# Partial sums of the first half leave PSUM through the four buffers of the weights' ring

## The chip, the cores and the metric

The kernel runs on one core of a Trainium2 chip. The metric is the time of one execution on the device, in microseconds (us). Before the change it is 872.65 us, the median of three runs (870.32, 872.65 and 874.05).

A core has these engines: TensorE (PE in the rows; PEld is its weight load), VectorE (DVE), ScalarE (ACT), GpSimd (POOL), and SyncE (SP), whose queue issues all DMAs here. Each engine carries out its own instructions in order; an instruction that waits for a semaphore holds all that stand behind it on that engine.

## The reference, cut to what matters

Sparse attention feeds two MLPs, one after the other, on 2304 tokens of width 512 with a hidden width of 2048:

```
x = attention(q, k, v)                          # 4 batches, 8 heads, 576 tokens, head width 64
h = x @ moe_w_in;  r = max(h, 0)
x = (moe_s * (r * r) + moe_b) @ moe_w_out       # first MLP
h = x @ moe2_w_in
g = h if h >= 1, 0 if h <= -1, else (h + 1)**2 / 4
out = g @ moe2_w_out                            # second MLP
```

The weights arrive as 64-bit floats and are decoded on the chip. Each fp32 operand of a product is split in a high and a low part (hi, lo), and each product is three matmuls: hi by hi, lo by hi, hi by lo.

## The kernel before, in words

The tokens are cut in six units of 384 (u = 0 to 5). The first MLP goes over the hidden width in two halves (`hf`), each of eight blocks of 128 (`m`). For one half, one unit and one block, `hidden` makes 12 matmuls into a PSUM tile `h` and a chain on ACT and DVE (relu L553, square L557 or L559, scale and shift L564 or L566, high part `gh` by the copy helper L282, low part `gl` L570). `output` makes 12 matmuls from `gh` and `gl` into four PSUM accumulators, three for each accumulator, in the order c = 0, 1, 2, 3. `output` of block m is issued two blocks behind `hidden` (LAG = 2), so on PE a group of 12 for `h` and a group of 12 for `acc` take turns.

The four accumulators (tags acc0 to acc3, one buffer each) hold the sum of one unit over the eight blocks of a half. Behind the last block of a unit in the first half, each is copied to SBUF by ACT (L282) or DVE (L284) into a tile `po` (L607, L608) and stored in DRAM as `part` (L609). Only then can the first matmul of the next unit write that accumulator. In the second half the parts are loaded back into tiles `pi` (L594) and added to the second half's sum (L613).

Behind the end of the attention (the list `lasts`), `prepare` makes the weights of the second MLP, beside the matmuls of the first. It decodes two blocks of weights (load L296, ACT L300, DVE L302, L304, L306) into tiles of the rings `qv` or `sm`, forms sums and differences of quarters (L365), and in `parts`, four times in each prepare, splits them: `hi` by ACT into a tile `pt` (L282), `lo` by DVE or POOL (L350); both are stored in DRAM as `dw` (L353). The first EARLY = 6 of the 16 prepares follow directly behind the attention, the others come in the second half.

Three rings of SBUF buffers matter here. `po` has PO = 2 buffers, `pi` has KD = 4, `pt` has PT = 2. A buffer is free when what was stored out of it has landed. Before the change `po` holds the parts of the first half and the low parts of the ten late prepares; `pi` holds the low parts of the six early prepares, and in the second half the parts that come back.

The order on each engine comes from a planner (`Issue.order`): every operation has a cost in us, a due time worked back from what needs it, and a fixed random jitter; the planner takes what can start first, then what is due first. An operation whose ring has no free buffer is not taken. A list given as `line=` (here `pi_line`) makes each of its operations start no earlier than the one before it on the list, which keeps the buffers of a ring in order.

Of the kernel before, what the change touches and what calls it, by code (L numbers as in the profile page):

```python
# [9 lines left out]
F32 = mybir.dt.float32  # L10
BF16 = mybir.dt.bfloat16
F32R = mybir.dt.float32r
# [10 lines left out]
KD = DM // 128  # L23
UNITS = [384] * 6
UMAX = max(UNITS)
# [17 lines left out]
RAW, DT, KB, QV, SM, PT, PO, TB = 3, 2, 4, 3, 3, 2, 2, 3  # L43
# [14 lines left out]
EARLY = 6  # L58
# [30 lines left out]
class Issue:  # L89
# [8 lines left out]
    def op(self, fn, engs, reads=(), writes=(), part=(), after=(), allocs=(), line=None):  # L98
        o = Op()
        o.fn, o.engs, o.n, o.succ, o.due = fn, engs, len(self.ops), [], None  # L100
        deps = set(after)
        o.behind, o.sooner = None, 0.0
        if line is not None:
            if line:
                o.behind = line[-1]
                deps.add(o.behind)
            line.append(o)
        for b in reads:
            deps.update(b.writers)
        for b in writes:  # L110
            deps.update(b.writers)
            deps.update(b.readers)
        for b in part:
            deps.update(b.readers)
        for b in reads:
            b.readers.append(o)
        for b in writes:
            b.writers, b.readers = [o], []
        for b in part:
            if b.readers:  # L120
                b.writers, b.readers = [], []
            b.writers.append(o)
        for b in allocs:
            b.writers = [o]
        o.deps = deps
        for d in deps:
            d.succ.append(o)
        o.bufs = [b for b in dict.fromkeys((*reads, *writes, *part, *allocs)) if b.ring]
        o.allocs = []
        for b in o.bufs:  # L130
            if not b.users:
                o.allocs.append(b)
                b.ring.made.append(b)
            b.users.append(o)
        self.ops.append(o)
        return o
# [85 lines left out]
def sparse_attention_two_mlps(ctx: ExitStack, tc: tile.TileContext, loc, strd, w_ins, w_outs, fixed, out):  # L222
# [5 lines left out]
    sp = ctx.enter_context(tc.tile_pool(name="sp", bufs=2))  # L228
# [19 lines left out]
    op = plan.op  # L248
# [4 lines left out]
    def buf(pool, tag, shape, dtype=F32, bufs=1):  # L253
        ring = rings.setdefault((pool.name if hasattr(pool, "name") else id(pool), tag), Ring(bufs))
        ring.name = tag
        serial[0] += 1
        name = f"{tag}_{serial[0]}"
        return Buf(ring, lambda: pool.tile(shape, dtype, tag=tag, name=name, bufs=bufs))


    def act(n):
        return ("act", 0.17 + n * 0.00062, 0.1)

    def dve(n, rate=0.00104):
        return ("dve", 0.07 + n * rate, 0.1)

    def dve2(n, rate=0.00104):

        return ("dve", 0.07 + n * rate, 0.1, "port")

    def pool(n):
        return ("pool", 0.1 + n * 0.0022, 0.1, "port")

    def dma(n, count=1):
        return ("sp", max(n / DMA_RATE, DMA_ISSUE * count), DMA_LATENCY)
# [4 lines left out]
    def copy(e, out, in_):  # L280
        if e is nc.scalar:
            e.activation(out=out, in_=in_, func=AF.Copy)  # L282
        else:
            e.tensor_copy(out=out, in_=in_)  # L284
# [4 lines left out]
    decodes, prepared, pi_line, w_loads, w0_line, w1_line = [], [], [], [], [], []  # L289
# [40 lines left out]
    def prepare(o, i):  # L330

        begin = len(plan.ops)
        src = w_outs if o else w_ins
        at = o * KP + i
        tag = ("qv", "sm")[at % 2]
        d1, d2 = (buf(sp, tag, [128, DM], I32, BUFS[tag]) for _ in range(2))
        _, x1, _, load = decode(src[2 * MS + i], lasts if at < EARLY else [*lasts, chain[0]], [d1, d2], d1)
        _, x2, *_ = decode(src[2 * MS + KP + i], [load], (), d2)
        where = {"A11": (d1, x1, 0), "A22": (d2, x2, 1)}
        where.update({"A21": (d1, x1, 1), "A12": (d2, x2, 0)} if o else {"A12": (d1, x1, 1), "A21": (d2, x2, 0)})  # L340

        def parts(b, f, k, names):
            n, q = 256 * len(names), [WMAT[name] for name in names]
            qs = slice(q[0], q[-1] + 1, max(q[-1] - q[0], 1))
            hi = buf(sp, "pt", [128, 512], F32R, PT)
            lo = buf(sp, "pi", [128, 512], F32R, KD) if at < EARLY else buf(sp, "po", [128, 512], F32R, PO)
            x = lambda: f()[:, k * 256:k * 256 + n]
            op(lambda e: copy(e, hi.tile[:, 0:n], x()), [act(n)], [b], [hi], allocs=[lo],
               line=pi_line if at < EARLY else None)
            op(lambda e: e.tensor_tensor(out=lo.tile[:, 0:n], in0=x(), in1=hi.tile[:, 0:n].bitcast(F32), op=SUB),  # L350
               [pool(n), dve2(n)], [b, hi], [lo])
            for w, y in enumerate((hi, lo)):
                op(lambda e, y=y, w=w: e.dma_start(  # L353
                    out=dw[o][i][qs, :, w, :].rearrange("q p n -> p q n"),
                    in_=y.tile[:, 0:n].bitcast(F32).rearrange("p (q n) -> p q n", n=256)), [dma(n * 512)], [y],
                   part=[dw_buf[o][i][v] for v in q])

        for names in [("A11",), ("A12", "A22")] if o else [("A11", "A12"), ("A22",)]:
            parts(*where[names[0]], names)

        for name, l, r, how in (("A22", "A21", "A22", ADD), ("A21", "A11", "A21", SUB), ("A11", "A22", "A11", SUB),
                                ("A12", "A12", "A11", SUB)):
            (b, f, k), (bl, fl, kl), (br, fr, kr) = (where[v] for v in (name, l, r))
            h = lambda f, k: f()[:, k * 256:(k + 1) * 256]
            op(lambda e, f=f, k=k, fl=fl, kl=kl, fr=fr, kr=kr, how=how: e.tensor_tensor(  # L365
                out=h(f, k), in0=h(fl, kl), in1=h(fr, kr), op=how), [dve2(256), pool(256)],
               [v for v in dict.fromkeys((bl, br)) if v is not b], [b])
        for names in [("S2", "S3"), ("S4", "S1")] if o else [("S2", "S4"), ("S3", "S1")]:
            parts(*((d1, x1) if names[0] == "S2" else (d2, x2)), 0, names)
        prepared.extend(plan.ops[begin:])  # L370
# [158 lines left out]
    def mm3(e, acc, w, x, first, last):  # L529
        (wh, wl), (ah, al) = w, x  # L530
        e.matmul(out=acc, lhsT=wh, rhs=ah, start=first, stop=False)  # L531
        e.matmul(out=acc, lhsT=wh, rhs=al, start=False, stop=False)  # L532
        e.matmul(out=acc, lhsT=wl, rhs=ah, start=False, stop=last)  # L533
# [4 lines left out]
    def pe_op(fn, n, reads, writes, allocs=()):  # L538
        chain[0] = op(fn, [pe(3 * (n / 2400 + 0.015))], reads, writes, after=[chain[0]] if chain[0] else (), allocs=allocs)
# [46 lines left out]
    def output(hf, u, m, g, gt):  # L586
        n = UNITS[u]
        w = wt[g, 1]
        cg = lambda: tuple(b.tile[:, 0:n] for b in gt)
        if hf == HF - 1 and m == 0:  # L590
            for c in range(KD):
                pin[c] = buf(sp, "pi", [128, UMAX], F32, KD)
                y = pin[c]
                op(lambda e, y=y, c=c: e.dma_start(out=y.tile[:, 0:n], in_=part_d[u][c]), [dma(n * 512)],  # L594
                   [part_buf[u][c]], [y], line=pi_line)
        for c in range(KD):
            if m == 0:
                acc[c] = buf(ps, f"acc{c}", [128, UMAX], F32, 1)
            a = acc[c]
            pe_op(lambda e, a=a, c=c: mm3(e, a.tile[:, 0:n], cut(w, c), cg(), m == 0, m == MS - 1), n, [*w, *gt], [a])  # L600
        if m < MS - 1:
            return
        line = []
        for c in range(KD):
            a = acc[c]
            if hf < HF - 1:
                y = buf(sp, "po", [128, UMAX], F32, PO)  # L607
                op(lambda e, y=y, a=a: copy(e, y.tile[:, 0:n], a.tile[:, 0:n]), [act(n), dve(n)], [a], [y])  # L608
                op(lambda e, y=y, c=c: e.dma_start(out=part_d[u][c], in_=y.tile[:, 0:n]), [dma(n * 512)],  # L609
                   [y], [part_buf[u][c]])  # L610
                continue
            y = pin[c]
            op(lambda e, y=y, a=a, c=c: e.tensor_tensor(out=x2[u].tile[:, c, :], in0=a.tile[:, 0:n], in1=y.tile[:, 0:n],  # L613
                                                        op=ADD),
               [dve(n)], [a, y], part=touched(u, c), allocs=[x2[u]] if c == 0 else (), line=line)
# [118 lines left out]
    n = NP  # L734
# [108 lines left out]
    at = 0  # L843
# [35 lines left out]
    for p in range(PAIRS):  # L879
        a = len(plan.ops)  # L880
# [110 lines left out]
```

## Time and profile before

| | |
|---|---|
| Median of three runs | 872.65 us (870.32 to 874.05) |
| Profiled execution | 872.29 us, its span 870.4 us |
| PE busy | 848.7 us (98%) |
| DVE, ACT busy | 663.5 us (76%), 533.9 us (61%) |
| Mean granted clock of TensorE | 0.984 of full speed |

The span runs from the first to the last instruction; 1.89 us of the profiled execution lie outside it. The attention's last matmuls are at about 170 us, the first half of the first MLP ends at about 323 us, the first MLP at about 517 us, and the second MLP takes the rest.

### The profile page before, as it was taken

How to read it: one execution, taken by the hardware profiler on the slowest of the kernel's cores; microseconds unless marked ns; L12 is line 12 of the kernel's file. 1: busy time of each engine (PE TensorE's matmuls, PEld its weight loads, DVE VectorE, ACT ScalarE, POOL GpSimd, SP SyncE). 2: the span in 40 equal slices, each digit the busy share in tenths (PEclk: the TensorE clock that was granted, in tenths of full speed). 3: DMA queues.
4: the chain of work that ended last, by engine and by line, in shares of the span. 5: the costliest groups of instructions: out<-in, count | busy, mean ns of one | idle time of the engine just before them, and what ended most of it. 6: DMA issues, size and time to landing. Idle time of an engine off the chain costs nothing.

```text
span 870.4 us, 15472 instructions
## 1 busy us (share of the span) xinstructions
PE 848.7 (98%) x5150; PEld 823.4 (95%) x5150; DVE 663.5 (76%) x1622; ACT 533.9 (61%) x1218; POOL 29.8 (3%) x43
## 2 busy tenths in 40 slices
PE   7799999998999999999999999999999999999998
PEld 4688898997999999999999999999999999999998
DVE  5899877588752892587988738899758998497966
ACT  5788776676654773566666635565555755465553
POOL 1112001000000000000000100000000000000000
PEclk9699999999899999999999999999999999999999
DMA  9568464478770560476878538888987888988783
GB/s 327 166 210 251 137 210 138 130 238 287 240 250 1 185 202 1 134 253 221 275 262 265 175 113 251 256 251 248 303 277 252 254 253 271 302 253 253 252 263 113
DMA packets 112591, 189.83 MB, mean 218 GB/s; under 512 B 11136, under 2 KB 54144, under 8 KB 112512
## 3 DMA queue, kind: packets, MB, share of 16 engines
q1 hardware_dynamic: 112512, 188.85, 67.9%
q8 instruction: 41, 0.67, 0.3%
q14 instruction: 38, 0.31, 0.1%
HBM read 150.00 MB, written 38.80 MB: 217 GB/s over the span
## 4 chain that ended last, share of the span: by engine, by line
PE 82%; DMA 8%; DVE 6%; ACT 2%; issue 1%; SPq 1%; DVEq 0%; ACTq 0%
PE acc L531 6%; PE acc L778 6%; PE h L531 6%; PE acc L779 6%; PE acc L777 6%; PE h L532 6%; PE h L533 6%; PE acc L532 6%; PE acc L533 6%; PE side L778 4%; PE side L779 4%; PE side L777 4%; PE h L778 3%; PE h L777 3%; PE h L779 3%; DMA raw<-in_w_ins 2%
## 5 line engine op out<-in xcount | busy, mean ns | idle before, releaser
L531 PE MATMUL acc<-gh,w1h 128*128 128x384 f32 x360 | 124.5, 346 | 5.8 <-ACT po L282 3.5
L532 PE MATMUL acc<-gl,w1h 128*128 128x384 f32 x360 | 121.2, 337 | 0.0
L533 PE MATMUL acc<-gh,w1l 128*128 128x384 f32 x360 | 121.1, 336 | 0.0
L531 PE MATMUL h<-xh,w0h 128*128 128x384 f32 x336 | 116.6, 347 | 0.0
L532 PE MATMUL h<-xl,w0h 128*128 128x384 f32 x336 | 114.4, 341 | 0.0
L533 PE MATMUL h<-xh,w0l 128*128 128x384 f32 x336 | 114.1, 339 | 0.0
L553 ACT ACTIVATE t<-h 128x384 f32<-128x384 f32 x96 | 46.4, 483 | 68.8 <-PE h L533 68.7
L531 PEld LDWEIGHTS acc<-gh,w1h 128*128 128x128 f32 x360 | 67.9, 189 | 8.6 <-ACT po L282 4.7
L532 PEld LDWEIGHTS acc<-gl,w1h 128*128 128x128 f32 x360 | 67.9, 189 | 0.1
L533 PEld LDWEIGHTS acc<-gh,w1l 128*128 128x128 f32 x360 | 67.8, 188 | 0.0
L531 PEld LDWEIGHTS h<-xh,w0h 128*128 128x128 f32 x336 | 64.3, 192 | 0.9 <-issue 0.5
L570 DVE TENSOR_TENSOR gl<-t,gh 128x384 fp32r<-128x384 f32 x92 | 51.0, 554 | 18.0 <-ACT gh L282 17.7
L532 PEld LDWEIGHTS h<-xl,w0h 128*128 128x128 f32 x336 | 64.4, 192 | 0.0
L533 PEld LDWEIGHTS h<-xh,w0l 128*128 128x128 f32 x336 | 64.2, 191 | 0.0
L566 DVE TENSOR_SCALAR t<-t,fix_t 128x384 f32<-128x384 f32 x58 | 29.7, 513 | 43.9 <-ACT t L557 43.7
L282 ACT ACTIVATE gh<-t 128x384 fp32r<-128x384 f32 x96 | 50.0, 521 | 18.3 <-DVE t L566 17.4
L282 ACT ACTIVATE gh<-w1h 128x384 fp32r<-128x384 f32 x60 | 31.6, 527 | 30.1 <-PE side L779 11.5
L456 ACT ACTIVATE sm<-sm,mx 128x96 f32<-128x96 f32 (+2 forms) x104 | 38.4, 372 | 11.2 <-DVE mx L446 10.9
L557 ACT ACTIVATE t<-t 128x384 f32<-128x384 f32 x76 | 39.8, 524 | 2.1
L819 DVE TENSOR_TENSOR gl<-w1h,gh 128x384 fp32r<-128x384 f32 x60 | 33.0, 553 | 6.7 <-ACT gh L282 6.7
L564 ACT ACTIVATE t<-t,fix_t 128x384 f32<-128x384 f32 x38 | 26.9, 708 | 3.2 <-DVE t L559 2.1
L282 ACT ACTIVATE pt<-sm 128x512 fp32r<-128x512 f32 (+1 forms) x32 | 18.2, 572 | 13.8 <-DVE sm L306 7.3
(342 smaller groups left out, 2342.7 us busy)
## 6 DMA issues: line engine op xcount, KB each, us to landing
w0h<-dw SPq DMA_DIRECT2D x168, 256.0 KB, 3.1
w0l<-dw SPq DMA_DIRECT2D x168, 256.0 KB, 3.1
raw<-in_w_ins SPq DMA_DIRECT2D x32, 512.0 KB, 5.0
raw<-in_w_outs SPq DMA_DIRECT2D x32, 512.0 KB, 4.5
dw<-pt SPq DMA_DIRECT2D x48, 256.0 KB, 3.1
dw<-po SPq DMA_DIRECT2D x30, 256.0 KB, 3.0
part<-po SPq DMA_DIRECT2D x24, 192.0 KB, 2.8
dw<-pi SPq DMA_DIRECT2D x18, 256.0 KB, 3.6
```

Source lines behind the costliest of these rows:

```text
L282: e.activation(out=out, in_=in_, func=AF.Copy)
L456: e.activation(out=sm.tile[0:nq, a, 0:nk], in_=sm.tile[0:nq, a, 0:nk], func=AF.Exp, scale=-1.0, bias=mx.tile[0:nq, a:a + 1], accum_out=dn. ...
L531: e.matmul(out=acc, lhsT=wh, rhs=ah, start=first, stop=False)
L532: e.matmul(out=acc, lhsT=wh, rhs=al, start=False, stop=False)
L533: e.matmul(out=acc, lhsT=wl, rhs=ah, start=False, stop=last)
L553: op(lambda e: e.activation(out=c(t), in_=c(p), func=AF.Relu), [act(n)], [p], [t])
L557: e.activation(out=c(t), in_=c(t), func=AF.Square)
L570: op(lambda e: e.tensor_tensor(out=c(gl), in0=c(t), in1=c(gh).bitcast(F32), op=SUB), [pool(n)] + [dve2(n)], [t, gh], [gl])
L777: e.matmul(out=dst, lhsT=wh, rhs=ah, start=opens and first, stop=False, skip_group_check=not opens)
L778: e.matmul(out=dst, lhsT=wh, rhs=al, start=False, stop=False, skip_group_check=not opens)
L779: e.matmul(out=dst, lhsT=wl, rhs=ah, start=False, stop=last, skip_group_check=not opens)
L819: op(lambda e, g=g, hi=hi, lo=lo: e.tensor_tensor(out=lo.tile, in0=g.tile, in1=hi.tile.bitcast(F32), op=SUB), [pool(n), dve2(n)], [g, hi], ...
```

## The change

The parts of the first half go into tiles of the ring `pi` (four buffers) and are put on `pi_line`. The low parts of the early prepares go into tiles of the ring `po` (two buffers), as those of the late ones do already, and leave `pi_line`. What is computed, the number of instructions and the sizes of all tiles stay.

```diff
@@ parts, in prepare @@
             hi = buf(sp, "pt", [128, 512], F32R, PT)
-            lo = buf(sp, "pi", [128, 512], F32R, KD) if at < EARLY else buf(sp, "po", [128, 512], F32R, PO)
+            lo = buf(sp, "po", [128, 512], F32R, PO)
             x = lambda: f()[:, k * 256:k * 256 + n]
-            op(lambda e: copy(e, hi.tile[:, 0:n], x()), [act(n)], [b], [hi], allocs=[lo],
-               line=pi_line if at < EARLY else None)
+            op(lambda e: copy(e, hi.tile[:, 0:n], x()), [act(n)], [b], [hi], allocs=[lo])
@@ output @@
             if hf < HF - 1:
-                y = buf(sp, "po", [128, UMAX], F32, PO)
-                op(lambda e, y=y, a=a: copy(e, y.tile[:, 0:n], a.tile[:, 0:n]), [act(n), dve(n)], [a], [y])
+                y = buf(sp, "pi", [128, UMAX], F32, KD)
+                op(lambda e, y=y, a=a: copy(e, y.tile[:, 0:n], a.tile[:, 0:n]), [act(n), dve(n)], [a], [y], line=pi_line)
                 op(lambda e, y=y, c=c: e.dma_start(out=part_d[u][c], in_=y.tile[:, 0:n]), [dma(n * 512)],
                    [y], [part_buf[u][c]])
```

Since the planner sees other rings, the order moves between the attention's last tiles and the end of the first half; outside of it the engines' rows stay. All lines behind L349 move up by one.

The first place is ACT at the end of unit 2 in the first half, near 210 us. There `acc_337` to `acc_340` are the accumulators c = 0 to 3 of that unit, `t` and `gh` belong to the chain of the next unit's blocks, `pt`, `sm` and `qv` to the prepares. Before:

```order
L300 ACTIVATE sm_2767<-raw_2766 128x512
L553 ACTIVATE t_2793<-h_2792 128x384
L282 ACTIVATE po_2828<-acc_337_2440 128x384
L557 ACTIVATE t_2793<-t_2793 128x384
L282 ACTIVATE po_2836<-acc_338_2447 128x384
L282 ACTIVATE pt_2842<-qv_2629 128x512
L282 ACTIVATE gh_2794<-t_2793 128x384
L282 ACTIVATE pt_2860<-qv_2630 128x512
L300 ACTIVATE sm_2768<-raw_2816 128x512
L553 ACTIVATE t_2848<-h_2847 128x384
L282 ACTIVATE po_2889<-acc_339_2456 128x384
```

Now:

```order
L300 ACTIVATE sm_2751<-raw_2750 128x512
L282 ACTIVATE pt_2805<-qv_2673 128x256
L552 ACTIVATE t_2792<-h_2791 128x384
L282 ACTIVATE pi_2828<-acc_337_2446 128x384
L556 ACTIVATE t_2792<-t_2792 128x384
L282 ACTIVATE pt_2838<-sm_2751 128x512
L282 ACTIVATE pi_2845<-acc_339_2458 128x384
L282 ACTIVATE pi_2856<-acc_340_2468 128x384
L282 ACTIVATE gh_2793<-t_2792 128x384
```

The copy of c = 2 stood behind the next block's relu and now stands two rows behind the copy of c = 0 and the square between them, with one `pt` copy ahead of it. The copy of c = 3 came from DVE and c = 1 from ACT; now it is the other way round.

The second place is DVE in the same stretch. The rows `pi<-..,pt` (before) and `po<-..,pt` (now) are low parts, `gl` is what PE waits for. Before, ahead of the end of unit 2:

```order
L350 TENSOR_TENSOR pi_2727<-sm_2395,pt_2726 128x512
L302 TENSOR_SCALAR qv_2630<-qv_2630 128x512
L350 TENSOR_TENSOR pi_2737<-sm_2396,pt_2736 128x512
L570 TENSOR_TENSOR gl_2692<-t_2690,gh_2691 128x384
L304 SCALAR_TENSOR_TENSOR qv_2630<-raw_2686,qv_2630 128x512
L306 SCALAR_TENSOR_TENSOR qv_2630<-raw_2686,qv_2630 128x512
L350 TENSOR_TENSOR pi_2775<-qv_2629,pt_2774 128x512
L566 TENSOR_SCALAR t_2741<-t_2741,fix_t 128x384
L350 TENSOR_TENSOR pi_2787<-qv_2630,pt_2786 128x256
```

Now, the closest run of low parts, ahead of the end of unit 3 (`acc_453` is its c = 1):

```order
L569 TENSOR_TENSOR gl_3098<-t_3096,gh_3097 128x384
L349 TENSOR_TENSOR po_3146<-qv_2968,pt_3145 128x512
L349 TENSOR_TENSOR po_3174<-qv_2967,pt_3173 128x512
L565 TENSOR_SCALAR t_3149<-t_3149,fix_t 128x384
L569 TENSOR_TENSOR gl_3151<-t_3149,gh_3150 128x384
L349 TENSOR_TENSOR po_3208<-sm_3038,pt_3207 128x256
L364 TENSOR_TENSOR sm_3038<-sm_3038 128x256
L364 TENSOR_TENSOR sm_3038<-sm_3037,sm_3038 128x256
L284 COPY pi_3231<-acc_453_2886 128x384
L364 TENSOR_TENSOR sm_3037<-sm_3038,sm_3037 128x256
L565 TENSOR_SCALAR t_3193<-t_3193,fix_t 128x384
L349 TENSOR_TENSOR po_3235<-sm_3038,pt_3234 128x512
```

A low part shares its buffer with the fourth one ahead of it before, and with the second one ahead of it now: `po_3208` with `po_3146`.

The third place is the SP queue at the end of the first half, where the last unit's parts are stored and the first parts are loaded back. Before:

```order
L609 DMA part_89<-po_3946 128x384
L699 DMA w0l_3973<-dw_1_91 128x512
L699 DMA w0h_3983<-dw_0_90 128x512
L609 DMA part_89<-po_3985 128x384
L699 DMA w0l_4003<-dw_1_91 128x512
L609 DMA part_89<-po_4005 128x384
L594 DMA pi_4245<-part_85 128x384
```

Now:

```order
L608 DMA part_89<-pi_3938 128x384
L608 DMA part_89<-pi_3945 128x384
L608 DMA part_89<-pi_3960 128x384
L593 DMA pi_3982<-part_84 128x384
L698 DMA w0l_3990<-dw_1_91 128x512
L593 DMA pi_3999<-part_84 128x384
L593 DMA pi_4006<-part_84 128x384
L593 DMA pi_4017<-part_84 128x384
L698 DMA w0h_4023<-dw_0_90 128x512
```

The four loads of unit 0's parts (`part_84`) stood among the early prepares, at about 247 to 252 us; they now follow the last stores, whose buffers they take.

## Rows read from the trace of the kernel before

**Rows 1.** The page, part 1: busy time, share of the span, instructions.

```profile
PE 848.7 (98%) x5150; PEld 823.4 (95%) x5150; DVE 663.5 (76%) x1622; ACT 533.9 (61%) x1218; POOL 29.8 (3%) x43
```

**Rows 2.** Waits of PE from 150 us: us in total, times, longest.

```profile
PE acc L531 <- ACT po L282: 3.5, 2, 3.3
PE acc L531 <- DVE po L284: 2.3, 2, 1.2
```

**Rows 3.** PE timeline: start, us, line, operation, out<-in, shape [idle before <- releaser].

```profile
196.47 0.34 PE L531 MATMUL h<-xh,w0h 128*128 128x384 f32 x1
...
200.63 0.34 PE L531 MATMUL h<-xh,w0h 128*128 128x384 f32 x1
...
207.06 0.34 PE L532 MATMUL acc<-gl,w1h 128*128 128x384 f32 x1
...
211.55 0.34 PE L533 MATMUL acc<-gh,w1l 128*128 128x384 f32 x1
...
215.97 0.44 PE L531 MATMUL acc<-gh,w1h 128*128 128x384 f32 x1 [3.28 <-ACT po L282]
...
217.82 0.69 PE L531 MATMUL acc<-gh,w1h 128*128 128x384 f32 x1 [1.07 <-DVE po L284]
...
223.68 0.34 PE L531 MATMUL acc<-gh,w1h 128*128 128x384 f32 x1
```

**Rows 4.** ACT and DVE timeline at the end of unit 2.

```profile
210.56 0.48 ACT L282 ACTIVATE po<-acc 128x384 f32<-128x384 f32 x1
210.93 0.53 ACT L557 ACTIVATE t<-t 128x384 f32<-128x384 f32 x1
211.34 0.49 ACT L282 ACTIVATE po<-acc 128x384 f32<-128x384 f32 x1
211.71 0.64 ACT L282 ACTIVATE pt<-qv 128x512 fp32r<-128x512 f32 x1
...
215.42 0.49 ACT L282 ACTIVATE po<-acc 128x384 f32<-128x384 f32 x1 [0.34 <-DMA part<-po]
...
217.21 0.56 DVE L284 COPY po<-acc 128x384 f32<-128x384 f32 x1 [1.32 <-DMA part<-po]
```

**Rows 5.** The chain that ended last, around 212 us: start, us, what.

```profile
211.86 5.25 DMA part<-po
```

**Rows 6.** Windows: us; PE, PEld, DVE, ACT, POOL busy; clock; DMA share; GB/s.

```profile
212.00:214.00 2.00, 0.68 (x3) 0.36 (x3) 2.00 (x5) 1.29 (x3) 0.00 (x0) 1.00 0.96 347
...
216.00:218.00 2.00, 0.93 (x4) 0.61 (x5) 0.79 (x2) 1.19 (x3) 0.00 (x0) 0.68 0.91 352
218.00:222.00 4.00, 4.00 (x13) 4.00 (x14) 3.79 (x9) 1.88 (x4) 0.00 (x0) 0.50 0.96 281
...
174.00:230.00 56.00, 51.64 (x279) 50.50 (x278) 46.89 (x94) 39.08 (x78) 0.00 (x0) 0.94 0.78 248
250.00:300.00 50.00, 48.52 (x278) 47.88 (x277) 23.43 (x44) 25.04 (x47) 0.00 (x0) 1.00 0.38 129
```

**Rows 7.** PE timeline at the ends of units 3 and 4.

```profile
253.76 0.44 PE L531 MATMUL acc<-gh,w1h 128*128 128x384 f32 x1 [0.24 <-ACT po L282]
...
288.61 0.44 PE L531 MATMUL acc<-gh,w1h 128*128 128x384 f32 x1 [1.24 <-DVE po L284]
```

**Rows 8.** DVE timeline: two low parts, two places apart, and a gl.

```profile
203.20 0.68 DVE L350 TENSOR_TENSOR pi<-sm,pt 128x512 fp32r<-128x512 f32 x1
...
204.85 0.55 DVE L570 TENSOR_TENSOR gl<-t,gh 128x384 fp32r<-128x384 f32 x1
...
206.65 0.68 DVE L350 TENSOR_TENSOR pi<-qv,pt 128x512 fp32r<-128x512 f32 x1
```

**Rows 9.** The tile pi from 174 to 232 us: issue to landing.

```profile
DMA to landing us min/median/max: 2.2/4.4/5.8
```

**Rows 10.** Waits of ACT from 174 to 250 us: us in total, times, longest.

```profile
ACT pt L282 <- DMA dw<-pt: 0.3, 1, 0.3
```

**Rows 11.** DVE timeline: the first use of the parts that come back.

```profile
351.46 2.15 DVE L613 TENSOR_TENSOR x<-acc,pi 128x384 f32<-128x384 f32 x4 [2.00 <-PE acc L533]
```

## The prediction

> **What bounds the kernel now.** I read the busy times first: PE is busy 98% of the span [rows 1], so only what makes PE idle, or its matmuls slow, can move the time by much. Next the waits of PE. From 150 us to the end PE waits almost only for one thing: at L531, the first matmul into an accumulator, for a copy into `po`. It is 3.5 us behind ACT's copies and 2.3 us behind DVE's, in four waits, 5.8 us in all [rows 2]. Three of the waits are at unit ends: 3.28 and 1.07 us at the end of unit 2 [rows 3], 0.24 us at unit 3 and 1.24 us at unit 4 [rows 7]; the sum is 5.83 us.
>
> Third, the timeline there shows why. At the end of unit 2 ACT copies c = 0 at 210.56 and c = 1 at 211.34 us, at once. The copies of c = 2 and c = 3 start at 215.42 and 217.21, and both rows name the store `part<-po` as what ended the wait [rows 4]: with two buffers the third copy needs the first store landed. The chain shows one of these stores taking 5.25 us from 211.86 [rows 5], with the DMA engines busy for 0.91 to 0.96 of that stretch [rows 6].
>
> Fourth, the windows show a second cost that no wait names: behind the gap the granted clock is 0.50 from 218 to 222 us, which is 1.2 of 2.4 GHz, while PE is busy all the time [rows 6]. PE ran at full clock before the gap, and was idle for 3.28 us and soon again for 1.07 us.
>
> **The price of the stall at unit 2.** At full speed 24 matmuls, from the row at 196.47 to the one at 200.63, take 4.16 us, 0.1733 us each. From 211.55 (the third matmul of c = 0) to 223.68 (the fourth of the next `acc` group) are 25 steps: 9 matmuls of c = 1 to 3, 12 for `h`, 3 for c = 0, and one more [rows 3]. They should take 25 x 0.1733 = 4.33 us and took 12.13. The loss is 7.80 us: 4.35 us of idle time, and 3.45 us of low clock and refilled pipeline.
>
> **The change, part by part.**
>
> *The copies go to four buffers.* A unit has four copies, and the next unit's come one unit later, over 30 us at this pace (192 matmuls x 0.1733 = 33 us) against a landing of 5.25 us [rows 5]. So no copy waits for a store any more. That takes away the 7.80 us at unit 2, and 0.24 + 1.24 = 1.48 us at units 3 and 4 [rows 7]. The lower bound for unit 2 is the idle time alone, 4.35 us, if something else should hold the clock down; the upper one is 7.80. I take 7.80, since the low clock followed the long gap: those of 0.24 and 1.24 us left it at 1.00 from 250 to 300 us [rows 6, 7].
>
> *What is late next at unit 2.* The copies must still be on time. The `gl` matmul at 207.06 us is the second of its group [rows 3]; 24 steps later is 211.22, so without a stall c = 0 is wanted at 211.05 and c = 2 six steps later, at 212.09. In the new order ACT has copy c = 0, the square, a `pt` copy, copy c = 2, copy c = 3. With the starts of before, 210.56, then 0.37 us to the square and 0.41 us behind it [rows 4], the `pt` copy starts at 211.34; it lasts 0.64 us, about 0.1 us of which the next one overlaps, as the rows beside it do. So copy c = 2 starts near 211.87 and ends near 212.36, and PE waits 0.3 us. c = 3 ends 0.4 us later, within the three matmuls of c = 2 (0.52 us). c = 1 is on DVE between short operations.
>
> *The `pt` copy ahead of c = 2* is the new danger: it waits for its own ring of two. Before, such waits were 0.3 us in all between 174 and 250 us [rows 10]. Its cost lies between nothing and a whole landing, 5.25 us [rows 5], less what has passed. I take 0.5 us, near the row.
>
> *Early low parts with two buffers.* There are 24 of them. The trace of before has no such wait, so I bound it. In before's order, the low part at 206.65 is the second behind that at 203.20 [rows 8]; its buffer would be free at 203.20 + 0.68 + 4.4 (median landing, rows 9) = 208.3 at the earliest: DVE would be held 1.6 us, at the largest landing of 5.8 us 3.0 us. What is queued behind is `gl`, and PE waits for `gl`: the one at 204.85 ends at 205.40 and is used at 207.06, so it has 1.66 us to spare [rows 3, 8]. But the order is new. In it the closest pair is `po_3146` and `po_3208`, with three DVE instructions between, one of them the `gl` of the next block. PE takes 24 matmuls a block, so `gl` come 4.16 us apart, and so about does this pair, against the 0.7 + 4.4 us that the buffer needs: a hold of 1 us, inside the spare 1.66 us. Other pairs stand farther apart. The bounds for all 24 are 0 and 24 x 1.6 = 38 us of DVE time; I take 0.4 us on PE, near the lower end, since each low part also waits for its high part, whose ring of two was enough before [rows 10]. The cover is the spare time of `gl`; if it is gone, each further us of DVE is a us of PE.
>
> The Trainium skill speaks of this price, in "DMA: Bandwidth & Descriptors", section "Anatomy of one DMA": a transfer costs about 2.0 us and its bytes over 436 GB/s, fitted on another issuing path. By that, as an estimate, a store of 256 KB lands in 2.6 us, and no low part would ever be held; the trace differs, 4.4 us in the middle [rows 9], and the measurement decides. For the store of 192 KB that held PE it gives 2.45 us against 5.25 us [rows 5]; with 2.45 us the stall would have been too short to be worth a change.
>
> *The loads of unit 0's parts* now follow the last stores, and the first must wait for one of these to land. On SP that is a hold of up to 5.25 us near 323 us, with only prefetched `w0h` and `w0l` tiles of the second MLP behind it. Their first use is at 351.46 us [rows 11], so 20 us are to spare: nothing. The skill says, on the same page and in the same section, that such a wait stands on the issuing sequencer, ahead of all it would issue next; that rule speaks against the change, and no run so far shows its price here.
>
> *The `pi_line`* only keeps the copies in order c = 0 to 3, as PE frees them: nothing.
>
> **Sum.** 872.29 (profiled) - 7.80 - 1.48 + 0.3 + 0.5 + 0.4 = 864.2. The median of the runs is 0.36 us above the profiled one, so 864.6 us, 0.9% less.
>
> **Rivals.**
>
> A. *ACT takes over the hold.* The `pt` copy ahead of c = 2, or a decode ahead of c = 0, waits for a DMA, and PE still idles some 3 us at unit 2, with the low clock behind it. For it: DMA is over 0.9 busy just there [rows 6], and landings reach 5.8 us [rows 9]. Against: ACT's waits on that ring were 0.3 us [rows 10]. Then half of the 7.80 comes back: 864.6 + 3.9 = 868.5; with a shorter gap without the low clock, 867.
>
> B. *DVE becomes the bound.* From 174 to 230 us DVE is busy 46.89 of 56 us [rows 6]. Take PE's 7.80 us out and the same work has 48.2 us: 97%, if none moves. DVE is in order, so what it is late with, PE waits for. For it: that share. Against: the low parts need not be done by then, the new order has 10 of the 24 ahead of unit 2's copies on DVE where 12 stood, and from 250 to 300 us DVE is busy only 23.43 of 50 us [rows 6]. If DVE keeps its 9.1 us of idle time, unit 2's gain is gone, and only units 3 and 4 give: 872.65 - 1.48 = 871.2.
>
> C. *Slower: low parts hold DVE at their ring.* The place is L349 between 180 and 250 us, the price 1.6 us for each of the 24 that comes too early, 3.0 at worst [rows 8, 9]. DVE's idle time there is 9.1 us; with eight holds it is used up, and each further one delays `gl`. With sixteen held, 16 x 1.6 - 9.1 = 16.5 us go to PE, against 9.3 us gained: 879.9. It decides the sign from about twelve holds. Against: the planner knows the ring, and has set the low parts apart.
>
> **How the numbers follow.** Forecast 0.70, A 0.14, B 0.11, C 0.05. About 0.5%, 4.4 us, is what a measurement can tell from no change, so faster means under 868.3: the forecast and most of A, 0.82; the rest of A and B are same, 0.13; C slower, 0.05. The range: below, the sum without new waits is 863.4 at the median, and the runs of before scatter 2.3 us below theirs: 861. Above, A at 868.5 and a little scatter: 869. That leaves out B and C, some 0.16.
>
> **What would show it.** Right: in the waits of PE no `po` or `pi` copy with over 1 us in all; no wait of ACT or DVE for `part`; granted clock 1.00 between 210 and 230 us; PE busy time some 3 us less. DVE's waits for `dw<-po` at L349 under 5 us, and none of PE for `gl`. Wrong for A: a wait of PE for ACT's copy at unit 2, with ACT's `pt` waiting for `dw<-pt` ahead of it. Wrong for B and C: waits of PE at L532 for `gl`, behind a DVE without idle time (B) or with long waits for `dw<-po` (C).

## The result, and the profile after

The changed kernel took 861.85 us in the median of 4 runs (858.77 to 866.6), beside 871.49 us for the kernel before in 4 runs on the same chip (869.62 to 874.05). The ratio is 0.9891, with an interval of 0.9848 to 0.9934: 9.6 us, or 1.1%, faster. Forecast were 864.6 us, between 861 and 869. The profiled execution took 861.83 us with a span of 859.6; before it was 872.29 and 870.4.

First, the head of the page after, which answers to the busy times of before [rows 1] (engine, busy us, share of the span, instructions):

```profile
span 859.6 us, 15474 instructions
PE 843.8 (98%) x5150; PEld 821.0 (96%) x5150; DVE 661.9 (77%) x1621; ACT 534.6 (62%) x1218; POOL 29.3 (3%) x44
PEclk9799999999999999999999999999999999999999
```

PE does the same 5150 matmuls in 4.9 us less busy time, and the span is 10.8 us shorter. So about half of the gain is time in which PE stood, and the other half time in which it worked slowly. Behind the second slice the granted clock is 0.9 or more everywhere.

From 150 us to the end the table of PE's waits is empty after the change; the two rows for copies into `po` [rows 2] have no successor. Next the windows of after (us; PE, PEld, DVE, ACT, POOL busy; clock; DMA share; GB/s), which answer to [rows 6]:

```profile
216.00:218.00 2.00, 2.00 (x14) 2.00 (x13) 0.95 (x3) 0.42 (x1) 0.00 (x0) 1.00 0.60 210
218.00:222.00 4.00, 4.00 (x25) 4.00 (x24) 2.97 (x7) 2.31 (x5) 0.00 (x0) 1.00 0.76 218
174.00:230.00 56.00, 56.00 (x325) 56.00 (x324) 49.17 (x99) 39.83 (x79) 0.00 (x0) 1.00 0.83 270
250.00:300.00 50.00, 50.00 (x290) 50.00 (x289) 29.41 (x56) 30.56 (x57) 0.00 (x0) 1.00 0.36 122
```

The reader is to see three things. PE is busy in all of the 56 us, where it was idle for 4.4 us. The clock from 218 to 222 us is 1.00, where it was 0.50. And DVE rose to 49.17 of 56 us, 88%, without becoming what PE waits for.

The same 25 matmul steps that took 12.13 us in before [rows 3] are between these two rows of PE's timeline after (start, us, engine, line, operation):

```profile
211.20 0.34 PE L532 MATMUL acc<-gh,w1l 128*128 128x384 f32 x1
...
215.54 0.34 PE L530 MATMUL acc<-gh,w1h 128*128 128x384 f32 x1
```

They take 4.34 us, which is the full-speed time of 4.33: the loss of 7.80 us is gone whole. How the copies come in time is seen in ACT's and DVE's timelines there, to be held beside [rows 4]:

```profile
207.04 0.66 ACT L300 ACTIVATE sm<-raw 128x512 f32<-128x512 f32 x1
...
208.28 0.47 ACT L282 ACTIVATE pi<-acc 128x384 f32<-128x384 f32 x1
...
210.14 0.63 ACT L282 ACTIVATE pt<-sm 128x512 fp32r<-128x512 f32 x1 [0.97 <-DVE sm L306]
210.68 0.85 ACT L282 ACTIVATE pi<-acc 128x384 f32<-128x384 f32 x2
...
216.86 0.42 ACT L282 ACTIVATE pt<-sm 128x256 fp32r<-128x256 f32 x1 [1.02 <-DMA dw<-pt]
```

```profile
210.35 0.55 DVE L284 COPY pi<-acc 128x384 f32<-128x384 f32 x1
```

c = 0 is copied at 208.28 (before: 210.56), c = 1 by DVE at 210.35, c = 2 and c = 3 in one row of two from 210.68. None waits for a store. The decode (`sm<-raw`, L300) stands ahead without a wait. Before, a decode in that place waited 1.34 us for its load, and held c = 0 with it:

```profile
209.63 0.66 ACT L300 ACTIVATE sm<-raw 128x512 f32<-128x512 f32 x1 [1.34 <-DMA raw<-in_w_ins]
```

How much of the old hold was the store? ACT reached c = 2's copy late in any case: behind c = 1's copy stood two `pt` copies, a `gh` and one more decode, which waited for its load too:

```profile
214.03 0.67 ACT L300 ACTIVATE sm<-raw 128x512 f32<-128x512 f32 x1 [0.75 <-DMA raw<-in_w_ins]
214.61 0.47 ACT L553 ACTIVATE t<-h 128x384 f32<-128x384 f32 x1
```

ACT was done with these at 215.08 us, and the store held c = 2's copy for only 0.34 us more [rows 4]. So of PE's 3.28 us about a tenth is ACT's wait for a store, and the rest is what the planner had put ahead of the copy, which it takes only once it reckons a buffer of the ring free. At c = 3 it is the store: DVE waited 1.32 us for it.

**Where the 10.8 us between the two spans came from.** I set the k-th matmul of after beside the k-th of before, each timed from its own first matmul. After leads by 0.2 us ahead of the end of unit 2 and by 8.1 us behind it: 7.9 us there. It leads by 8.6 us behind unit 3 and by 10.2 us behind unit 4: 2.05 us from these two. At the end of the first half come 0.4 us more, and 0.5 near 457 us, where PE waited 0.2 us for a sum (`x`, L613) in before [rows 2]. That is 11.1 us; some 0.3 are lost again in the last stage.

### The profile page after: what moved, and what is told of

It reads as the page before. It is cut to its first block, busy times and chain, and to the rows that moved or that the text cites. A ratio compares the mean times of both kernels' runs of the same rounds, so it can differ in the third digit from the quotient of the medians.

```text
span 859.6 us, 15474 instructions
## 1 busy us (share of the span) xinstructions
PE 843.8 (98%) x5150; PEld 821.0 (96%) x5150; DVE 661.9 (77%) x1621; ACT 534.6 (62%) x1218; POOL 29.3 (3%) x44
## 4 chain that ended last, share of the span: by engine, by line
PE 93%; DMA 3%; DVE 3%; ACT 0%; issue 0%; SPq 0%; POOL 0%; ACTq 0%
PE h L530 8%; PE h L531 8%; PE acc L530 8%; PE h L532 8%; PE acc L532 7%; PE acc L531 7%; PE acc L777 6%; PE acc L776 6%; PE acc L778 6%; PE side L777 5%; PE side L776 5%; PE side L778 5%; PE h L777 3%; PE h L778 3%; PE h L776 3%; PE side L432 2%
```

## The experiments

Each run was timed beside runs of the kernel before on the same chip; ratios are to those. Three questions are asked: which part of the change does it, is it the buffers or the order, and is the low clock a consequence of the idle time.

**1. The low parts alone go to `po`; the partial sums stay there too.**

```
-lo = buf(sp, "pi", [128, 512], F32R, KD) if at < EARLY else buf(sp, "po", [128, 512], F32R, PO)
+lo = buf(sp, "po", [128, 512], F32R, PO)       (and no pi_line on the copy of hi)
```

> One half of the change: the early low parts go to po (two buffers), the parts stay in po as well. If low parts in two buffers cost nothing by themselves and only the parts' four buffers help: parts and low parts wait for each other's stores, PE's waits for copies grow over the 5.8 us of before, 873 to 880 us. If the move of the low parts is what helps: under 868 us.

Measured: 883.19 us (4 runs), ratio 1.011 (1.0082 to 1.0138), slower than either theory said. PE's waits from 150 us on (for what: us in total, times, longest):

```profile
PE acc L530 <- ACT po L282: 7.5, 3, 5.2
PE acc L530 <- DVE po L284: 2.9, 2, 1.6
```

Ten us of waits where 5.8 stood: the early low parts and the partial sums now share two buffers, which leaves still less of the ring to the sums. (Before the change the sums had the ring `po` to themselves in the first half: the late low parts come into it only from 363 us.)

**2. The partial sums alone go to `pi`; the early low parts stay there.**

```
-y = buf(sp, "po", [128, UMAX], F32, PO)
+y = buf(sp, "pi", [128, UMAX], F32, KD)       (and line=pi_line on the copy)
```

> The other half of the change: the parts go to pi (four buffers, on its line), the early low parts stay in pi as well. If four buffers are enough even when shared: 862 to 865 us. If the parts have to be apart from the early low parts, a copy waits for low parts' stores and the line holds copies back: PE waits of 2 to 6 us at unit ends, 866 to 873 us.

Measured: 893.35 us (4 runs), ratio 1.0241 (1.0214 to 1.0268), the slowest of all, and beyond both ranges expected, which end at 873:

```profile
PE acc L531 <- DVE pi L284: 22.5, 1, 22.5
```

One copy of a partial sum on DVE, at 301.30 us, came 22.5 us late. The line keeps one order for all that uses the ring, and low parts stood ahead of it: those, done by 250 us after the real change, ran on beyond 300 us here, with DVE busy for 43.97 of the 50 us before. The copy itself waited for no store: DVE came to it without idling, so it is the order forced by the common line that cost this, not a full ring. Four buffers shared without a line were not run. The two halves of the change are each slower by themselves and faster together.

**3. The order of before, to the instruction, but the partial sums in four buffers.** The planner goes on seeing the ring of two; only the memory behind it alternates between two pairs.

```
-y = buf(sp, "po", [128, UMAX], F32, PO)
+y = buf(sp, "po", [128, UMAX], F32, PO, real=(("po", "pa")[c % 2], 2))
```

> The planner sees the rings of before, so every engine has the order of before; but the parts get four real buffers (two of po for c = 0 and 2, two of their own for c = 1 and 3), and no part waits for a store of its own unit. Theory B, the number of buffers alone is the cause: no wait for part stores is left and PE's waits for po copies fall from 5.8 us to under 0.5, about 863 us, nearly the time of the changed kernel. Theory O, the order that follows from the rings does most of it: the copy of c = 2 still stands on ACT behind two pt copies, a gh and a decode that waits for its load (started at 214.0 us before), so PE still waits 2 to 3 us at the end of unit 2, with the low clock behind it, while units 3 and 4 lose their 1.5 us: 866 to 870 us.

Measured: 872.34 us (10 runs), ratio 0.9999 (0.9974 to 1.0023): no gain in the time of the whole, and above the ranges of both theories. The waits for `part` are gone, but c = 2's copy has another one ahead of it. ACT's timeline, and the matmul that waits:

```profile
212.01 0.66 ACT L301 ACTIVATE sm<-raw 128x512 f32<-128x512 f32 x1 [1.06 <-DMA raw<-in_w_ins]
212.57 0.48 ACT L554 ACTIVATE t<-h 128x384 f32<-128x384 f32 x1
212.94 0.49 ACT L283 ACTIVATE po<-acc 128x384 f32<-128x384 f32 x1
```

```profile
213.48 0.45 PE L532 MATMUL acc<-gh,w1h 128*128 128x384 f32 x1 [2.52 <-ACT po L283]
```

The old order puts a decode, which waits for its load, between c = 0 and c = 2. PE stood 2.52 us, the clock stayed at 1.00, and 4.8 of the 7.9 us at unit 2 were still gained in this profile, and 1.4 at units 3 and 4. So the buffers alone did gain, by 6.2 us in the first half. It then lost 4.0 us near 450 us, in the second half: waits of 1.72 and 0.94 us for the sum `x`, with a spell of low clock behind them (0.66 from 450 to 455 us). What these come from is said under "What stays open".

**4. The order of after, but the partial sums in two buffers.**

```
-y = buf(sp, "pi", [128, UMAX], F32, KD)
+y = buf(sp, "pi", [128, UMAX], F32, KD, real=("pa", 2))
```

> The planner sees the rings of the change, so every engine has the order of the changed kernel; but the parts get only two real buffers, of their own. Theory B: copies of c = 2 and 3 wait for the stores of c = 0 and 1; these are issued near 209 us and land 3 to 5 us later, so PE, which wants c = 2 at 212.1 us, waits 0 to 2 us at unit 2 and some tenths at others, ACT is held behind the copy, and the time is 864 to 869 us. Theory O: the copies now come 2 us earlier, the stores land nearly in time, and it stays within 2 us of the changed kernel, 860 to 864 us.

Measured: 875.83 us (10 runs), ratio 1.0042 (1.0021 to 1.0063), above the 860 to 869 us of both theories. The profile is of the slowest of the ten (880.47 us). ACT's copies are held by the stores, and for longer than the old ones:

```profile
215.63 0.49 ACT L283 ACTIVATE pi<-acc 128x384 f32<-128x384 f32 x1 [1.20 <-DMA part<-pi]
...
218.59 0.49 ACT L283 ACTIVATE pi<-acc 128x384 f32<-128x384 f32 x1 [2.46 <-DMA part<-pi]
```

So the new order is no gain by itself. The 25 steps at the end of unit 2 put the two experiments side by side: 12.13 us before, 7.50 with the buffers alone (210.11 to 217.61), 11.23 with the order alone (212.87 to 224.10), 4.34 with both. Buffers and order go together: the planner, told of four buffers, sets the copies where four buffers serve them.

**5. How many buffers.** The partial sums get a ring of their own that the planner knows, of two and of three.

```
-y = buf(sp, "pi", [128, UMAX], F32, KD)
+y = buf(sp, "pa", [128, UMAX], F32, 2)        (3 in the other run; no pi_line)
```

> The changed kernel, but the parts have a ring of their own with two buffers that the planner knows, not on a line; the early low parts are in po with two, as in the change. Theory B+O (it takes four buffers and the order that the planner makes of them): the wait for a part's store of the same unit is back at the ends of units 2 to 4, 870 to 877 us. Rival (it is enough that the parts are apart from pi and its line): under 866 us.

> As the one with two buffers of their own, with three: the copy of c = 2 is free, only c = 3 waits for the store of c = 0. Theory B+O: at unit 2 PE wants c = 3 some 4 us behind the first copy, about what a store takes, so most of the loss goes: 863 to 868 us. Rival: as two buffers, over 870 us.

Measured: with two 873.35 us (10 runs), ratio 1.0003 (0.9983 to 1.0023); with three 865.91 us (5 runs), 0.9912 (0.9884 to 0.9941). PE's waits, first with two, then with three:

```profile
PE acc L530 <- ACT pa L282: 4.4, 4, 2.6
```

```profile
PE acc L530 <- ACT pa L282: 1.9, 2, 1.2
```

Two of their own are worth nothing, which is as it should be: two to themselves is what the sums had in the first half of before. So it is not worth anything by itself that the low parts left `pi`; the depth is needed. Most of the gain comes with the third buffer; with the fourth no wait for a copy is left. With two the clock fell again (0.59 from 216 to 223 us), with three it did not (1.00 from 210 to 220 us).

**6. Is the low clock a consequence of the idle time, or of the load there?** The order of before, with 18 and 5 matmuls of zeros added where PE stood at the end of unit 2, ahead of c = 2 and of c = 3.

```
+for _ in range(zeros):     # {2: 18, 3: 5} by c, at the first block of unit 3 alone
+    e.matmul(out=b.tile[:, 0:n], lhsT=warm_t[:, 0:128], rhs=warm_t[:, 0:n], start=False, stop=False)
```

> The kernel before, with the same order; only in the first block of unit 3, PE runs 18 matmuls of zeros (added to the accumulator c = 1, which they leave as it is) ahead of the matmuls of c = 2, and 5 ahead of c = 3, so PE is busy where it idled for 3.28 and 1.07 us. Theory: the low clock behind the gap comes from PE being idle. Then the granted clock is 1.00 from 205 to 230 us, the loss at unit 2 falls from 7.8 to 5 us, and the time is 869 to 871 us. Rival: the low clock comes from the load of that stretch (DMA and vector engine busy) and not from the idle time: 0.50 stays, the loss stays near 7.8 us or grows, 872 to 874 us.

Measured: 872.36 us (10 runs), ratio 0.9988 (0.9967 to 1.0008). Its windows, to be held beside before's, where the clock from 215 to 220 us is 0.67:

```profile
210.00:215.00 5.00, 5.00 (x32) 3.94 (x31) 3.93 (x8) 4.06 (x9) 0.00 (x0) 1.00 1.02 345
215.00:220.00 5.00, 5.00 (x31) 4.39 (x30) 4.55 (x10) 2.57 (x6) 0.00 (x0) 1.00 0.93 298
```

```profile
210.00:215.00 5.00, 2.68 (x14) 1.85 (x12) 4.29 (x9) 4.25 (x10) 0.00 (x0) 1.00 1.06 337
215.00:220.00 5.00, 2.97 (x10) 2.65 (x11) 3.50 (x7) 3.40 (x8) 0.00 (x0) 0.67 0.90 321
```

The DMA share is the same (1.02 and 0.93, against 1.06 and 0.90), and the clock stays up while PE is kept busy: the load of that stretch does not lower it. The rest of the record agrees: in all fourteen profiles every stretch of low clock between 165 us and the last matmuls begins in a gap of PE or right behind one. Less is shown of the gap that the zeros filled. The copies came sooner here than in before:

```profile
212.71 3.10 PE L604 MATMUL acc<-warm_t 128*128 128x384 bf16 x18
215.51 0.47 PE L531 MATMUL acc<-gh,w1h 128*128 128x384 f32 x1
```

```profile
213.71 0.49 ACT L282 ACTIVATE po<-acc 128x384 f32<-128x384 f32 x1 [0.19 <-DMA part<-po]
```

c = 2's copy was done at 214.20 us, so without zeros PE would have stood some 1.5 us and not 3.28, and whether the clock had fallen behind that is not known. Nor does the run give the price of the low clock: the 25 steps lose 3.8 us here instead of 7.80, but that is the length of the zeros and their refill. The price is read from before [rows 3]: the 18 steps from 217.82 to 223.68 took 5.86 us where 3.12 are due, so 2.7 of the 3.45 us are low clock and the other 0.7 refill behind gaps. The time of the whole lies in the rival's range. Of the 4.1 us gained at unit 2, 3.6 went near 455 us, in the same place as in experiment 3; 1.2 us that went at the end of unit 3, where this profile has a wait of 1.46 us, came back at unit 4.

**7. The changed kernel again, and both kernels with another seed of the planner.** The seed (L41) draws another order; the kernels are otherwise the same.

```
-SEED, JITTER = 521290, 1.0
+SEED, JITTER = 521291, 1.0
```

> The changed kernel once more, for a second profile: its four times so far lie from 858.8 to 866.6 us. Expected: no wait of PE for a copy at the ends of units 2 to 4 in this run either; and if the time is over 863 us, a wait for the sum L612 near 445 us (end of unit 2 in the second half) with a low clock behind it, as in the runs with the old order or two buffers near 455 us. If it is under 863 us, none there.

> The kernel before with the next seed of the planner's jitter, so another order with the same rings. Theory: PE waits 4 to 8 us for copies of the parts at unit ends as before, 869 to 878 us. Rival (the gain was a lucky order): it lies anywhere, also under 866 us.

> The changed kernel with the same next seed. Theory: no wait of over 1 us for copies of the parts, 6 to 12 us faster than the kernel before with that seed, 860 to 867 us. Rival (a lucky order): no faster than the kernel before with that seed.

Measured: again 864.65 us (3 runs, 864.5 to 864.78), ratio 0.9898 (0.9865 to 0.9931). The wait for the sum that was expected with such a time is there, but it is 0.3 us and no low clock follows, so it is not what makes these runs slower than 861.85. With the other seed, before 873.94 (8 runs), 0.9994 (0.997 to 1.0018), and after 866.64 (4 runs), 0.9914 (0.9874 to 0.9953). So the gain is 7.3 us in another order: not the luck of one. Before with the other seed still waits for the copies, and after does not:

```profile
PE acc L531 <- DVE po L284: 4.5, 3, 3.3
```

```profile
PE side L436 <- DMA kb<-in_loc: 1.4, 1, 1.4
PE acc L530 <- DVE x L612: 0.9, 1, 0.9
```

**8. Or does the planner only reckon the stores too short?** It takes a landing as 2.2 us and the bytes over a rate; the stores of partial sums landed in 2.8 us in the middle, and in 5.25 us at the one that held c = 3's copy [rows 5].

```
-DMA_LATENCY = 2.2
+DMA_LATENCY = 2.8
```

> The kernel before with the planner's latency at 2.8 us. Theory B+O: with two buffers for the parts no order takes away the landing of c = 0's store ahead of c = 2's copy, so PE's waits for copies stay over 3 us in all, 868 to 874 us. Rival (the rings did not matter, only the planner's wrong latency did): PE's waits for copies under 1 us, 861 to 866 us.

> The changed kernel with one number of the planner's: a DMA's latency of 2.8 us where it had 2.2. The traces show landings of 3 to 5 us behind 180 us, so the planner was too hopeful. Theory: what is left near 450 us (a wait of PE for the sum L612, with a low clock behind it where it is long) comes from decodes that the planner puts too early for their loads; with 2.8 us it is gone, and the time is 858 to 862 us with less spread, also under the changed kernel in the worse of its runs (864.7). Rival: any new order is a draw; 860 to 868 us.

Measured: before with this line alone, two buffers as they were, 865.15 us (4 runs), ratio 0.9892 (0.9858 to 0.9926); after with it 861.16 us (4 runs, 858.71 to 862.48), 0.9843 (0.98 to 0.9887). Before's ACT and PE at the end of unit 2 are now:

```profile
206.53 0.48 ACT L282 ACTIVATE po<-acc 128x384 f32<-128x384 f32 x1
...
210.34 1.04 ACT L282 ACTIVATE po<-acc 128x384 f32<-128x384 f32 x2 [0.94 <-DMA part<-po]
```

```profile
210.88 0.44 PE L531 MATMUL acc<-gh,w1h 128*128 128x384 f32 x1 [1.35 <-ACT po L282]
```

I had thought that no order could take away this loss with two buffers. That fell, for most of it: the time lies in the rival's range. c = 0 is copied 4.0 us sooner than in before, while PE is 2.7 us ahead there; c = 2 follows 3.8 us behind c = 0, where it was 4.9 [rows 4]. PE's hold is 1.35 us and not 3.28, and the clock from 206 to 216 us is 1.00. No decode that waits for a load stands ahead of either copy any more. PE's waits for copies are still 3.1 us in all, as expected, 0.48 and 1.23 of them at units 3 and 4, which gain nothing; and 2.7 of the 8.2 us by which this profile leads come from the attention, ahead of all copies. The 25 steps take 6.01 us. So two causes stand beside each other, a ring that is short and a planner that reckons DMAs too fast. The line changes loads and stores alike, and this run doesn't tell which of them matters. Either cure alone gives most of the gain. Both together have the lowest median of the study, 861.16 us, ahead of before with the 2.8 alone (865.15); the plain change (858.77 to 866.6) is not told apart from it.

## Why the prediction was right, point by point

- **The mechanism** held in its main line: a ring of two made PE wait for copies, and the clock fell behind that wait. Experiments 4 and 5 bring the waits back with two buffers, and in 6 the clock stays up under the same load while PE is busy. But the prediction gave the whole hold at c = 2 to the store, and ACT waited only 0.34 us for it; with four buffers and the old order PE still stood 2.52 us of the 3.28 (experiment 3). That the full 7.80 us went is due to the new order as much as to the buffers; the prediction did go through that order, and found it to be in time but for the terms below.
- **Unit 2:** 7.80 forecast, 7.9 found. The split, 4.35 idle and 3.45 of low clock and refill, is a reading of before's rows; experiment 6 neither confirms nor moves it.
- **Units 3 and 4:** 1.48 forecast, 2.05 found. The term took only the idle time. For unit 2 the steps had been counted from matmul to matmul, which takes in the refill behind a gap; here they had not been.
- **The new waits**, +0.3 for c = 2's copy, +0.5 for the `pt` copy, +0.4 for the low parts: this is the term that was mis-sized. They cost PE nothing. The first two were worked out by setting the new order on the start times of the old one (c = 0 at 210.56). But 210.56 was itself late, behind a decode that waited for its load, and in the new order c = 0 starts at 208.28. ACT's waits for the `pt` ring did grow, from 0.3 us [rows 10] to 2.5 us in all, but the long ones, at 216.86 and 218.16, stand behind c = 3's copy, where nothing of PE's hangs on them.
- **The low parts in two buffers** held nobody. From 174 to 232 us their landings are 1.8, 3.3 and 6.4 us (least, middle, most), against 2.2, 4.4 and 5.8 in before [rows 9]. The estimate by the Trainium skill ("DMA: Bandwidth & Descriptors", "Anatomy of one DMA"), 2.6 us, is still 0.7 below the middle and 3.8 below the longest. Where the landing was the longest, 6.39 us, the order left time enough. At the pair that the prediction took as the closest, `po_3146` and `po_3208`, it was the landing:

```profile
239.39 1.28 DVE L349 TENSOR_TENSOR po<-qv,pt 128x512 fp32r<-128x512 f32 x2
242.33 0.43 DVE L349 TENSOR_TENSOR po<-sm,pt 128x256 fp32r<-128x256 f32 x1
```

  The two are 2.94 us apart and not 4.16, so a landing of 4.4 would have held DVE for 2 us; the store took 2.14 us and landed 0.1 us ahead of the second. The +0.4 was saved by a short landing there, which is luck as far as the prediction goes.
- **The loads of unit 0's parts:** on SP the wait for the last stores was 0.3 us, not up to 5.25. They are issued from 312.3 to 314.7 us and first used at 340.89, so it cost nothing.
- **Rivals.** A, that ACT takes over the hold, did not come with the change, but it is just what the old order does when it is given four buffers (experiment 3): a real danger, which the new order avoids. B, DVE as the bound: it is busy for 88% of the stretch and late with nothing. C did not come: the low parts make no one wait when they have two buffers to themselves. (Its sum has a slip: at 1.6 us each, six holds use up 9.1 us, not eight.)

The sum without the new waits is 863.0 on the profiled time; with the 0.57 of units 3 and 4, the 0.1 of unit 2, the 0.9 not foreseen behind them and the 0.3 lost at the end it comes to 861.7; less the 0.2 us of the time ahead of unit 2, 861.5. The profiled run took 861.83, of which 0.3 us is that the time around its span is longer (2.2 us against 1.9).

**What stays open.** Near 445 to 460 us PE waits for the sum `x`: 0.2 us in the profile of before, 0 and 0.3 in the two of after, but 1.6 to 2.7 us in experiments 3, 4 and 6 (and 0.8 to 1.5 in 1 and 5 and with the other seed). There it takes 3 to 4 us with its low clock, and hides what was gained earlier. The traces of 3, 4 and 6 show the chain. ACT's decode waits 1.06 to 1.60 us for its load, DVE's part of that decode stands ahead of the sum, and PE waits for the sum; in experiment 3:

```profile
446.63 0.66 ACT L301 ACTIVATE sm<-raw 128x512 f32<-128x512 f32 x1 [1.22 <-DMA raw<-in_w_outs]
```

```profile
447.33 0.43 DVE L303 TENSOR_SCALAR sm<-sm 128x512 int32<-128x512 int32 x1 [1.33 <-ACT sm L301]
449.13 1.01 DVE L614 TENSOR_TENSOR x<-acc,pi 128x384 f32<-128x384 f32 x2
```

That load landed in 5.6 to 5.8 us in these three, and in 4.4 to 5.0 in before and the two of after. Both profiles with 2.8 us are without the wait, and in their order this decode stands behind the sum, as the last expectation has it. Why the same load lands later in some runs stays open.

## What to carry to other kernels

When an accumulator waits for its eviction and that for a store, count the buffers from the landing time that the trace shows under the load of that stage, not from the usual one; and let nothing else fill the ring of the evictions (experiment 1 is slower for it). Look at what is queued ahead of the eviction too: a deeper ring left PE 2.52 of 3.28 us of waiting while the old order kept a waiting decode in front of the copy, and an order planned with a longer landing time gained most of it without a deeper ring. When a piece of the program is re-ordered, do not carry start times over from the old trace without asking what they had waited for.

## What the runs showed of the hardware

- Short waits are not alike for the clock, and their length alone does not say what follows. Single gaps of 2.52 us (experiment 3) and 1.35 us (experiment 8) left it at 1.00, while a single one of 2.06 us (experiment 1) brought 0.58 from 262 to 266 us, and one of 3.27 us (before with the other seed) 0.57 from 218 to 222 us. Gaps of 3.28 and 1.07 us, close behind each other, brought 0.50 from 218 to 222 us (before), and 1.72 and 0.94 us 0.66 from 450 to 455 us (experiment 3); 0.73 and 1.18 us left it at 1.00 (experiment 5, three buffers).
- The landing of the same stores differs with the order around them: those of the partial sums went from 1.9, 2.8 and 5.3 us (least, middle, most) to 1.9, 2.8 and 3.8 in the changed order, with the same bytes.
- Single profiles of the changed kernel differ by 3 us (861.83 and 864.78) though the loss at unit 2 is taken away in both: 1.0 us comes from the first 150 to 200 us and the rest from behind 450 us, and no wait for a copy is in either.
